# Attention into a Sinkhorn-routed expert layer: the last group's tiles in their own width, second-layer weights loaded by whole rows, five experts' weights in the first batch

## The chip, the cores and the metric

The kernel runs on one core of a Trainium2 chip. The metric is the device time of one execution in microseconds (us); several executions are timed, and the median is given. A further execution is recorded by the hardware profiler; every view of the profile and every duration below come from that one. The engines are TensorE (PE; its weight loads are shown apart as PEld), VectorE (DVE), ScalarE (ACT), GpSimd (POOL) and SyncE (SP). SP, ACT and POOL also issue transfers, each on a DMA queue of its own (q1 for SP, q10 for ACT, q0 for POOL), and all three queues run on the same 16 DMA engines.

## The reference, cut to what matters

Attention with a local window and 32 global tokens gives x, 4352 rows (8 batches x 544 positions) of 512. A small gate gives one weight per row and expert, made even over rows and columns in eight rounds. Then eight experts of two layers each are applied to all rows:

```python
    logits = x @ w_gate                      # (4352, 512) @ (512, 8)
    P = np.exp(logits - logits.max())
    for _ in range(8):
        P /= P.sum(1, keepdims=True) + 1e-09
        P /= P.sum(0, keepdims=True) + 1e-09
        P *= N / E
    for e in range(E):                       # E = 8
        h = np.maximum(x @ w1[e], 0.0)       # 512 -> 1024
        ye = h @ w2[e]                       # 1024 -> 512
        out += P[:, e:e + 1] * ye
```

The inputs are float32; the kernel computes in float16 with float32 sums.

## The kernel before, in words

**Rows and groups.** The 4352 rows are cut into nine groups m of 512, 512, ..., 256: groups 0 to 7 hold the local rows of one batch each, and the last group, m = 8 (B in the code), the 8 x 32 global rows. Activations are kept transposed, a feature in a partition and a row in a column. xT is x in this form.

**First stretch, to about 334 us: attention** for 32 pairs of heads, and mixed into it, as filling for PE, the first layer of experts 0 to 3 (`p_l1`, L459): for each group and expert eight blocks `fm` of four matmuls (L466), evicted with a relu by ACT or DVE into a tile hT of [128, 8, 512] from the pool hpool, which has four buffers. A finished tile is stored to DRAM (hd, L473) by SP, or by ACT in the second stretch. The weights w2 of the second layer are not needed yet.

**Second stretch, about 334 to 400 us.** PE still has first-layer tiles to do: `tail_run` hands them out between the rounds that make the gate even (`sk_rows`, `sk_cols`, on DVE and PE). The last four are those of group 8, experts 0 to 3 in turn; they use 256 of the 512 columns of their tile. POOL loads w2 of four experts (`load_w2c`, L665), with a cast from float32 to float16 in the transfer, and DVE makes sums of quarters (`prep_w2c`, L674).

**Third stretch, about 400 us to the end: 72 units (m, e)**, the groups in turn and in each the experts in the order ORDER = 4, 0, 5, 1, 6, 2, 7, 3. Units are numbered i from 0. An even unit is an expert of 4 to 7: its first layer is computed here (`l1`, L730: w1s from DRAM, xs is x scaled by the gate's weights pb, `scale_x`), and ACT evicts into a tile h of hpool (L738). An odd unit is an expert of 0 to 3: its h is loaded from hd by SP (`load_h`, L718) into a buffer of the same pool and scaled by DVE (`scale_h`). DVE forms `sums` of the halves of h, and PE does the second layer as seven products q of quarter blocks (`product`, L759) where eight would be the plain way. PSUM holds five of the products over all experts of a group (ps_fix); the products 6 and 7 are summed over two units in buffers of ps_rot, which has three, and added to the output tile o after each odd unit (`add`, L784; by ACT for unit 1 of a group, else by DVE, L795). The other l1 blocks use ps_rot too.

**Order.** The order of the instructions on each engine is written out by hand; the framework adds the semaphores. A buffer of a pool goes to the next tile that asks, and that tile's first writer waits for the last reader of the old one. For hpool that reader is the store of a group-8 tile. The order on DVE in the main loop matters below: at an even i it is sums(i+1), scale_x(i+4), prep_w2c of one expert (only in group 0: expert 6 at i = 0, 2 at i = 2, 7 at i = 4, 3 at i = 6), scale_h(i+3); at an odd i it is sums(i+1), then the additions. On SP: w1s of unit i+5 at an odd i; pb of units i+3 and i+4, x where a new group starts, and h of unit i+3 at an even one.

**Second-layer weights.** w2c[e] holds seven blocks of [128, 4, 256] for an expert: the four quarters of w2 and sums of them. Six experts have their tile in the pool wc, the last two of ORDER (7 and 3) in wr, which takes the place of xT once the first layer is through. After `tail_run`, POOL waits for the first group-8 tile by copying a few of its elements into a small tile `mark` (L907), then loads expert 6; a second copy into mark (L916) waits for unit 0's tile, then POOL loads experts 2, 7 and 3:

```python
    mark = wr.tile([P, 2, 2], FP16, name="mark")
    nc.gpsimd.tensor_copy(out=mark[:, 0], in_=hTs[(0, B)][:, FT - 1, 0:2])
    load_w2c(6)
```

Of the kernel before, what the change touches and what calls it, by code (L numbers as in the profile page):

```python
# [9 lines left out]
FP16 = mybir.dt.float16  # L10
FP32 = mybir.dt.float32
AF = mybir.ActivationFunctionType
ALU = mybir.AluOpType
# [10 lines left out]
def kernel(  # L24
# [13 lines left out]
    nc = tc.nc  # L38
# [51 lines left out]
    with tc.tile_pool(name="att_c", bufs=1) as att_c, \  # L90
# [368 lines left out]
        def p_l1(e, m, fm, eng, pool=None, tag="mm"):  # L459
            n = groups[m][1]  # L460
            if fm == 0:
                hTs[(e, m)] = hpool.tile([P, FT, 512], FP16, tag="hT", name="hT")
            hT = hTs[(e, m)]
            ph = (pool or ps_mm).tile([P, 512], FP32, tag=tag, name="ph")
            for dk in range(DP):
                nc.tensor.matmul(ph[:, 0:n], wts[e][:, dk, P * fm : P * (fm + 1)], xT[m][:, dk, :],  # L466
                                 start=(dk == 0), stop=(dk == DP - 1))
            if eng == "a":
                nc.scalar.activation(out=hT[:, fm, 0:n], in_=ph[:, 0:n], func=AF.Relu)  # L469
            else:  # L470
                nc.vector.tensor_scalar(out=hT[:, fm, 0:n], in0=ph[:, 0:n], scalar1=0.0, scalar2=None, op0=ALU.max)  # L471
            if fm == FT - 1:
                (nc.scalar if pool else nc.sync).dma_start(out=hd[e][m], in_=hT[:, :, 0:n])  # L473

        def load_w1e(e):
            pool, kw = ((wpool, dict(tag="w1e")), (wpool, dict(tag="w1e")), (wpool, dict(tag="w2e", bufs=1)),
# [181 lines left out]
    wc = ctx.enter_context(tc.tile_pool(name="wc", bufs=1, reuse_waits="tile"))  # L658
    xsp = ctx.enter_context(tc.tile_pool(name="xsp", bufs=2, reuse_waits="tile"))
    ORDER = (4, 0, 5, 1, 6, 2, 7, 3)  # L660
    w2c = {e: wc.tile([P, 7, FT // 2, D // 2], FP16, name=f"w2c{e}") for e in ORDER[:6]}
    idf = wc.tile([P, P], FP32, name="idf")
    HF, HD = FT // 2, D // 2

    def load_w2c(e):  # L665
        w = w2c[e]
        for i, (f, d) in ((1, (0, 0)), (4, (1, 1)), (2, (0, 1)), (3, (1, 0))):
            nc.gpsimd.dma_start(out=w[:, i], in_=moe_w2[e][P * HF * f : P * HF * (f + 1), HD * d : HD * (d + 1)]
                                .rearrange("(fko fki) d -> fki fko d", fki=P))

    def tt(out, in0, in1, op):
        nc.vector.tensor_tensor(out=out, in0=in0, in1=in1, op=op)  # L672

    def prep_w2c(e):  # L674
        w = w2c[e]
        tt(w[:, 0], w[:, 1], w[:, 4], ALU.add)
        tt(w[:, 5], w[:, 1], w[:, 2], ALU.add)
        tt(w[:, 6], w[:, 3], w[:, 4], ALU.add)
        tt(w[:, 2], w[:, 2], w[:, 4], ALU.subtract)
        tt(w[:, 3], w[:, 3], w[:, 1], ALU.subtract)  # L680

    for e in ORDER[:4]:
        load_w2c(e)

    units = [(m, e) for m in range(B + 1) for e in ORDER]
# [14 lines left out]

    def load_x(m):
        if m <= B:
            xgs[m] = xsp.tile([P, DP, 512], FP16, tag="xg", name="xg")
            nc.sync.dma_start(out=xgs[m][:, :, 0 : groups[m][1]], in_=xd[m])

    def scale_x(i):
        if i < NUN:
            m = units[i][0]
            n = groups[m][1]
            xss[i] = xsp.tile([P, DP, 512], FP16, tag="xs", name="xs")  # L710
            tt(xss[i][:, :, 0:n], xgs[m][:, :, 0:n],
               pbs.pop(i)[:, 0:n].unsqueeze(1).to_broadcast([P, DP, n]), ALU.mult)

    def alloc_h(i):
        if i < NUN:
            hs[i] = hpool.tile([P, FT, 512], FP16, tag="hT", name="h")

    def load_h(i):  # L718
        if i < NUN:
            m, e = units[i]  # L720
            alloc_h(i)
            nc.sync.dma_start(out=hs[i][:, :, 0 : groups[m][1]], in_=hd[e][m])

    def scale_h(i):
        if i < NUN:
            n = groups[units[i][0]][1]
            h = hs[i][:, :, 0:n]
            tt(h, h, pbs.pop(i)[:, 0:n].unsqueeze(1).to_broadcast([P, FT, n]), ALU.mult)

    def l1(i, fm, pool, tag):  # L730
# [32 lines left out]
    def product(i, q):  # L763
        m, e = units[i]
        n = groups[m][1]
        nt = n // P // 2
        first = e == ORDER[0]
        h, s, w = hs[i], ss[i], w2c[e]
        lhs = {1: (s[:, 2], 0), 2: (s[:, 1], 0), 3: (h[:, 0:HF], 0), 4: (h[:, HF:FT], n // 2),
               5: (s[:, 0], 0), 6: (h[:, 0:HF], n // 2), 7: (h[:, HF:FT], 0)}[q]  # L770
        if q >= 6 and i % 2 == 0:
            pm = fixed[q] = ps_rot.tile([P, 512], FP32, tag="r", name="pm")
        elif first:
            pm = fixed[q] = ps_fix.tile([P, 512], FP32, tag=f"m{q}", name=f"m{q}")
        else:
            pm = fixed[q]
        for t in range(nt):
            for k in range(HF):
                nc.tensor.matmul(pm[:, HD * t : HD * (t + 1)], lhs[0][:, k, lhs[1] + P * t : lhs[1] + P * (t + 1)],  # L779
                                 w[:, q - 1, k, :], start=(k == 0 and t == 0 and (first if q < 6 else i % 2 == 0)),  # L780
                                 stop=(k == HF - 1 and (closes(i) if q < 6 else i % 2 == 1 or closes(i))),
                                 skip_group_check=True)

# [16 lines left out]
    def last_pair(i):  # L800
        m, e = units[i]
        o, h, w = os_[m], hs[i], w2c[e]
        n = groups[m][1]
        lo, hi = h[:, 0:HF, 0:n], h[:, HF:FT, 0:n]
        s = ss[i]
        for c in range(n // P):
            q = slice(P * c, P * (c + 1))
            pm = ps_rot.tile([P, 512], FP32, tag="r", name="pm")
            for d, terms in ((1, ((lo, 2), (s, 4))), (0, ((hi, 3), (s, 1)))):
                for t, (a, wi) in enumerate(terms):  # L810
                    for k in range(HF):
                        nc.tensor.matmul(pm[:, HD * d : HD * (d + 1)], a[:, k, q], w[:, wi, k, :],
                                         start=(d == 1 and t == 0 and k == 0),
                                         stop=(t == 1 and k == HF - 1), skip_group_check=True)
            nc.vector.scalar_tensor_tensor(out=o[:, c, :], in0=pm, scalar=1.0 / float(E), in1=o[:, c, :],  # L815
                                           op0=ALU.mult, op1=ALU.add)
            for b in range(4 * c, 4 * c + 4):
                eng = {3: nc.gpsimd, 7: nc.sync}.get(b, (nc.sync, nc.scalar)[c])
                eng.dma_start(out=out[S * b : S * b + Sg, :], in_=o[W * (b % 4) : W * (b % 4 + 1), c, :])  # L819
# [79 lines left out]
    load_pb(2)  # L899
    prep_w2c(1)  # L900
    scale_x(2)
    tail_run(1000)
    load_w1(2)
    psx.close()
    wr = ctx.enter_context(tc.tile_pool(name="wr", bufs=1, side="right", reuse_waits="tile"))
    mark = wr.tile([P, 2, 2], FP16, name="mark")
    nc.gpsimd.tensor_copy(out=mark[:, 0], in_=hTs[(0, B)][:, FT - 1, 0:2])  # L907
    load_w2c(6)
    for e in ORDER[6:]:
        w2c[e] = wr.tile([P, 7, FT // 2, D // 2], FP16, name=f"w2c{e}")  # L910
    alloc_h(0)
    load_h(1)
    for fm in range(FT):
        pool, tag = cyc[fm % 2]
        l1(0, fm, pool, tag)
    nc.gpsimd.tensor_copy(out=mark[:, 1], in_=hs[0][:, FT - 1, 0:2])  # L916
    for e in (2, 7, 3):
        load_w2c(e)
    load_w1(4)
# [5 lines left out]
    for i, (m, e) in enumerate(units):  # L925
        if i == NUN - 1:
            last_pair(i)
        elif i % 2 == 0:
            alloc_h(i + 2)
            load_pb(i + 3)  # L930
            load_pb(i + 4)
            if (i + 4) % E == 0:
                load_x((i + 4) // E)
            load_h(i + 3)
            if i + 2 < NUN:
                sums(i + 1)
            else:
                n = groups[m][1]
                h = hs[i + 1]
                s = ss[i + 1] = wpool.tile([P, HF, n], FP16, tag="w2e", name="sl", bufs=1)  # L940
                tt(s, h[:, 0:HF, 0:n], h[:, HF:FT, 0:n], ALU.add)
            scale_x(i + 4)
            if m == 0:
                for e in {0: (6,), 2: (2,), 4: (7,), 6: (3,)}.get(i, ()):
                    prep_w2c(e)
            scale_h(i + 3)
            for fm in range(3):
                l1(i + 2, fm, ps_rot, "r")
            for q, fm in ((3, 3), (4, 4), (5, 5), (2, 6), (1, 7), (6, None), (7, None)):
                product(i, q)  # L950
                if fm is not None:
                    l1(i + 2, fm, ps_rot, "r")
            if closes(i):
                for q in (6, 7, 3, 4, 5, 2, 1):
                    add(i, q, fixed[q])
        else:
            load_w1(i + 5)
            sums(i + 1)
            for q in (6, 7, 3, 4, 5, 2, 1):
                product(i, q)  # L960
                if q >= 6 or closes(i):
                    add(i, q, fixed[q])
            if closes(i):
                store(m)
# [31 lines left out]
```

## Time and profile before

| what | value |
|---|---|
| three executions | 1075.87, 1077.94, 1078.65 us; median 1077.94 |
| the profiled execution | 1076.82 us, of it the span 1075.0 us from the first to the last instruction |
| mean granted TensorE clock | 0.989 of full |
| busy share of the span | PE 96%, PEld 65%, DVE 75%, ACT 45%, POOL 14% |

Busy time by stretch (us):

| stretch | length | PE | DVE | ACT | POOL | granted clock | DMA share |
|---|---|---|---|---|---|---|---|
| 0 to 334 | 334 | 310.3 | 251.3 | 260.3 | 118.7 | 0.98 | 0.79 |
| 334 to 398 | 64 | 62.9 | 44.1 | 40.6 | 17.9 | 1.00 | 0.97 |
| 398 to 461 | 63 | 51.8 | 41.9 | 18.4 | 10.1 | 0.95 | 1.02 |
| 461 to 1075 | 614 | 605.1 | 471.3 | 169.5 | 0.5 | 1.00 | 0.45 |

A stretch is read by how much PE falls short of its length: 23.7 us in the first, 1.2 in the second, 11.2 in the third and 8.9 in the last. The DMA share is a mean over the 16 engines; transfers of several queues on one engine count side by side, so it can pass 1. A time of a matmul is from its issue to its modelled end, and matmuls overlap; what a matmul costs is the distance to the next one: 0.217 us for 512 columns at full clock, 0.109 for 256.

In the chain of work that ended last, everything from 438.84 us on is one entry, "issue", of 631 us: the profile shows nothing there that the last engine waited for long.

### The profile page before, as it was taken

Reading aid. Unit: us, or ns where it says so; the run is one execution under the profiler, and the core shown is the slowest. Engines: PE = TensorE matmul, PEld = TensorE weight load, DVE = VectorE, ACT = ScalarE, POOL = GpSimd, SP = SyncE. Lnnn points to the kernel's source line nnn. Section 1 sums busy time; section 2 is a strip of 40 time slices with the busy share of each in tenths; the row PEclk is TensorE's granted clock in tenths of the full one; section 3 lists DMA queues with packets and bytes.
Section 4 is the critical chain, followed back from the end, with each engine's and each line's share of the span. In section 5 each row is a group of like instructions: output and inputs, shape, how many; then the busy total and the mean of one; then the engine's idle time right before and its main releaser. Section 6 shows DMA issues by size and latency. Waiting matters only on the chain.

```text
span 1075.0 us, 21707 instructions
## 1 busy us (share of the span) xinstructions
PE 1030.0 (96%) x8854; PEld 701.1 (65%) x8854; DVE 808.6 (75%) x1464; ACT 488.8 (45%) x1248; POOL 147.1 (14%) x233
## 2 busy tenths in 40 slices
PE   7799999999999997989999999999999999999997
PEld 4455555555554463767777777777777777777786
DVE  8577777777775763998887877878777787678766
ACT  7668888787785663223223222223223233232231
POOL 7342423413404113000000000000000000000000
PEclk9899999999999998999999999999999999999999
DMA  9877588988947979954635435435335535535351
GB/s 269 191 187 202 114 262 202 212 239 178 218 147 185 275 231 207 274 167 139 196 116 187 167 104 194 154 138 196 128 127 196 174 116 179 199 118 180 110 169 52
DMA packets 113331, 190.82 MB, mean 178 GB/s; under 512 B 33680, under 2 KB 80736, under 8 KB 100432
## 3 DMA queue, kind: packets, MB, share of 16 engines
q1 hardware_dynamic: 58176, 159.61, 43.5%
q0 software_dynamic: 48912, 20.26, 15.4%
q10 hardware_dynamic: 6144, 9.57, 2.6%
q8 instruction: 69, 1.13, 0.4%
q14 instruction: 30, 0.25, 0.1%
HBM read 157.11 MB, written 53.62 MB: 196 GB/s over the span
## 4 chain that ended last, share of the span: by engine, by line
issue 61%; PE 21%; ACT 7%; DMA 5%; DVE 5%; POOL 0%; SPq 0%; ACTq 0%; POOLq 0%
PE ph L466 14%; ACT Pu L309 4%; DVE Pu L346 2%; DMA w2c<-in_moe_w_dram 2%; DMA hd<-hT 1%; PE ptw L357 1%; ACT hT L469 1%; ACT qbd L283 1%; DMA vraw<-in_v_l_dram 1%; DMA f<-in_q_l_dram 1%; PE pt L273 1%; DMA kgf<-in_k_g_dram 1%; PE pv L155 1%; PE po L378 1%; PE sc L299 1%
## 5 line engine op out<-in xcount | busy, mean ns | idle before, releaser
L738 ACT ACTIVATE h<-ph 128x512 f16<-128x512 f32 (+1 forms) x288 | 164.8, 573 | 419.6 <-PE ph L736 404.6
L736 PE MATMUL ph<-xs,w1s 128*128 128x512 f16 (+1 forms) x1152 | 272.5, 370 | 13.0 <-ACT h L738 6.5
L466 PE MATMUL ph<-xT,w1e 128*128 128x512 f16 (+1 forms) x1152 | 257.6, 368 | 1.9 <-ACT hT L469 1.7
L779 PEld LDWEIGHTS <-h 128*128 128x128 f16 x2160 | 211.4, 98 | 44.3
L672 DVE TENSOR_TENSOR s<-h 128x1024 f16<-128x1024 f16 (+2 forms) x142 | 124.0, 915 | 103.0 <-ACT h L738 59.5
L779 PE MATMUL m<-w2c,s 128*128 128x256 f16 x1620 | 199.9, 273 | 0.0
L779 PEld LDWEIGHTS <-s 128*128 128x128 f16 x1620 | 158.4, 98 | 38.3 <-DVE s L672 0.2
L736 PEld LDWEIGHTS <-w1s 128*128 128x128 f16 x1152 | 113.3, 98 | 98.4 <-issue 17.7
L466 PEld LDWEIGHTS <-w1e 128*128 128x128 f16 x1152 | 105.5, 98 | 98.4 <-issue 6.2
L672 DVE TENSOR_TENSOR h<-h,pb 128x4096 f16<-128x4096 f16 (+1 forms) x36 | 150.7, 4186 | 4.3 <-DMA h<-hd 4.1
L779 PE MATMUL m<-w2c,h 128*128 128x256 f16 x1080 | 135.2, 273 | 0.0
L469 ACT ACTIVATE hT<-ph 128x512 f16<-128x512 f32 (+1 forms) x191 | 103.2, 559 | 50.2 <-PE ph L466 46.4
L779 PE MATMUL pm<-w2c,h 128*128 128x256 f16 x1080 | 123.8, 273 | 0.0
L672 DVE TENSOR_TENSOR xs<-xg,pb 128x2048 f16<-128x2048 f16 (+1 forms) x36 | 78.1, 2171 | 48.6 <-DMA pb<-pd 42.4
L309 ACT ACTIVATE Pu<-ms,mx 128x160 f16<-128x160 f32 x224 | 93.5, 420 | 4.0 <-DVE mx L306 1.5
L471 DVE TENSOR_SCALAR hT<-ph 128x512 f16<-128x512 f32 x97 | 66.8, 689 | 31.4 <-PE ph L466 30.8
L819 POOL DMA_DIRECT2D out_dram<-o x1 | 0.5, 534 | 638.5 <-DVE o L815 638.5
L672 DVE TENSOR_TENSOR h<-h 128x1024 f16<-128x1024 f16 (+1 forms) x142 | 87.8, 661 | 0.0
L306 DVE CUSTOM_DVE_ANT_0 ms<-sc,mask 128x160 f32<-128x160 f32 x224 | 59.9, 320 | 24.8 <-PE sc L301 22.4
L350 POOL TENSOR_TENSOR Pl<-Pu,rs 128x256 f16<-128x256 f16 x32 | 24.4, 763 | 195.9 <-DVE rs L345 130.7
L795 DVE SCALAR_TENSOR_TENSOR o<-m,o 128x512 f32<-128x512 f32 (+1 forms) x72 | 43.2, 656 | 5.2 <-ACT o L793 2.1
L346 DVE TENSOR_TENSOR Pu<-Pu,rs 128x768 f16<-128x768 f16 x64 | 44.5, 696 | 2.2
(153 smaller groups left out, 954.4 us busy)
## 6 DMA issues: line engine op xcount, KB each, us to landing
w1s<-w1d SPq DMA_DIRECT2D x36, 1024.0 KB
h<-hd SPq DMA_DIRECT2D x32, 1024.0 KB
hd<-hT SPq DMA_DIRECT2D x26, 1024.0 KB
pb<-pd SPq DMA_DIRECT2D x64, 256.0 KB
w2c<-in_moe_w_dram POOLq DMA_DIRECT2D x32, 256.0 KB, 16.1
out_dram<-o SPq DMA_DIRECT2D x8, 1024.0 KB
f<-in_q_l_dram SPq DMA_DIRECT2D x15, 512.0 KB
f<-in_k_l_dram SPq DMA_DIRECT2D x15, 512.0 KB
```

The lines of the kernel that those rows point to most:

```text
L306: nc.vector.tensor_tensor_reduce(out=ms[:, ii, :], in0=sc[:, SW * ii : SW * (ii + 1)], in1=mask[:, mi, :], scale=-scale, scalar=BIG, op0=A ...
L309: nc.scalar.activation(out=d["Pu"][:, i, :], in_=ms[:, ii, :], func=AF.Exp, scale=-1.0, bias=d["mx"][:, i : i + 1], accum_out=d["sm"][:, i ...
L346: nc.vector.tensor_tensor(out=d["Pu"][:, i0:i1, 0:KW], in0=d["Pu"][:, i0:i1, 0:KW], in1=d["rs"][:, i0:i1].unsqueeze(2).to_broadcast([P, i1 ...
L350: nc.gpsimd.tensor_tensor(out=d["Pl"], in0=d["Pu"][:, :, KW:SW], in1=d["rs"].unsqueeze(2).to_broadcast([P, NHB, Sg]), op=ALU.mult)
L466: nc.tensor.matmul(ph[:, 0:n], wts[e][:, dk, P * fm : P * (fm + 1)], xT[m][:, dk, :], start=(dk == 0), stop=(dk == DP - 1))
L469: nc.scalar.activation(out=hT[:, fm, 0:n], in_=ph[:, 0:n], func=AF.Relu)
L471: nc.vector.tensor_scalar(out=hT[:, fm, 0:n], in0=ph[:, 0:n], scalar1=0.0, scalar2=None, op0=ALU.max)
L672: nc.vector.tensor_tensor(out=out, in0=in0, in1=in1, op=op)
L736: nc.tensor.matmul(ph[:, 0:n], w1s[i][:, dk, P * fm : P * (fm + 1)], xss[i][:, dk, 0:n], start=(dk == 0), stop=(dk == DP - 1))
L738: nc.scalar.activation(out=hs[i][:, fm, 0:n], in_=ph[:, 0:n], func=AF.Relu)
L779: nc.tensor.matmul(pm[:, HD * t : HD * (t + 1)], lhs[0][:, k, lhs[1] + P * t : lhs[1] + P * (t + 1)], w[:, q - 1, k, :], start=(k == 0 and ...
L795: nc.vector.scalar_tensor_tensor(out=o, in0=p, scalar=sg / float(E), in1=o, op0=ALU.mult, op1=ALU.add)
```

## The change

Four things.

1. The tiles hT of `p_l1`, h of `alloc_h` and x of `load_x` get the width of their group, n, in place of 512. Only group 8 differs (256). A tile's rows then follow each other without gaps, so a transfer of it moves one run of 4 KB per partition (h; 2 KB for x) where it moved eight (four) of 512 bytes.
2. The blocks of w2c[e] lie in another order, [128, 4, 7, 256], so that the two quarters of a half of w2 stand side by side. `load_w2c` makes two transfers per expert of whole rows (2 KB read, 1 KB written) in place of four of half rows. `prep_w2c` and the products read the same numbers from the new places.
3. The first batch of loads takes in a fifth expert, 6; the first copy into mark and the load behind it go.
4. prep_w2c(6) moves from unit 0 of the main loop to the place after scale_x(2), ahead of the last `tail_run`.

```diff
         def p_l1(e, m, fm, eng, pool=None, tag="mm"):
             n = groups[m][1]
             if fm == 0:
-                hTs[(e, m)] = hpool.tile([P, FT, 512], FP16, tag="hT", name="hT")
+                hTs[(e, m)] = hpool.tile([P, FT, n], FP16, tag="hT", name="hT")
...
             if fm == FT - 1:
-                (nc.scalar if pool else nc.sync).dma_start(out=hd[e][m], in_=hT[:, :, 0:n])
+                (nc.scalar if pool else nc.sync).dma_start(out=hd[e][m], in_=hT)
...
-    w2c = {e: wc.tile([P, 7, FT // 2, D // 2], FP16, name=f"w2c{e}") for e in ORDER[:6]}
+    w2c = {e: wc.tile([P, FT // 2, 7, D // 2], FP16, name=f"w2c{e}") for e in ORDER[:6]}
...
     def load_w2c(e):
         w = w2c[e]
-        for i, (f, d) in ((1, (0, 0)), (4, (1, 1)), (2, (0, 1)), (3, (1, 0))):
-            nc.gpsimd.dma_start(out=w[:, i], in_=moe_w2[e][P * HF * f : P * HF * (f + 1), HD * d : HD * (d + 1)]
-                                .rearrange("(fko fki) d -> fki fko d", fki=P))
+        for f in range(2):
+            nc.gpsimd.dma_start(out=w[:, :, 1 + 2 * f : 3 + 2 * f].rearrange("p k i d -> p k (i d)"),
+                                in_=moe_w2[e][P * HF * f : P * HF * (f + 1)].rearrange("(fko fki) d -> fki fko d", fki=P))
...
     def prep_w2c(e):
         w = w2c[e]
-        tt(w[:, 0], w[:, 1], w[:, 4], ALU.add)
-        tt(w[:, 5], w[:, 1], w[:, 2], ALU.add)
-        tt(w[:, 6], w[:, 3], w[:, 4], ALU.add)
-        tt(w[:, 2], w[:, 2], w[:, 4], ALU.subtract)
-        tt(w[:, 3], w[:, 3], w[:, 1], ALU.subtract)
-
-    for e in ORDER[:4]:
+        for o, a, b, op in ((0, 1, 4, ALU.add), (5, 1, 2, ALU.add), (6, 3, 4, ALU.add),
+                            (2, 2, 4, ALU.subtract), (3, 3, 1, ALU.subtract)):
+            tt(w[:, :, o], w[:, :, a], w[:, :, b], op)
+
+    for e in ORDER[:5]:
         load_w2c(e)
...
     def load_x(m):
         if m <= B:
-            xgs[m] = xsp.tile([P, DP, 512], FP16, tag="xg", name="xg")
-            nc.sync.dma_start(out=xgs[m][:, :, 0 : groups[m][1]], in_=xd[m])
+            xgs[m] = xsp.tile([P, DP, groups[m][1]], FP16, tag="xg", name="xg")
+            nc.sync.dma_start(out=xgs[m], in_=xd[m])
...
     def alloc_h(i):
         if i < NUN:
-            hs[i] = hpool.tile([P, FT, 512], FP16, tag="hT", name="h")
+            hs[i] = hpool.tile([P, FT, groups[units[i][0]][1]], FP16, tag="hT", name="h")
...
             alloc_h(i)
-            nc.sync.dma_start(out=hs[i][:, :, 0 : groups[m][1]], in_=hd[e][m])
+            nc.sync.dma_start(out=hs[i], in_=hd[e][m])
...
-                                 w[:, q - 1, k, :], start=(k == 0 and t == 0 and (first if q < 6 else i % 2 == 0)),
+                                 w[:, k, q - 1, :], start=(k == 0 and t == 0 and (first if q < 6 else i % 2 == 0)),
...
     prep_w2c(1)
     scale_x(2)
+    prep_w2c(6)
     tail_run(1000)
     load_w1(2)
     psx.close()
     wr = ctx.enter_context(tc.tile_pool(name="wr", bufs=1, side="right", reuse_waits="tile"))
-    mark = wr.tile([P, 2, 2], FP16, name="mark")
-    nc.gpsimd.tensor_copy(out=mark[:, 0], in_=hTs[(0, B)][:, FT - 1, 0:2])
-    load_w2c(6)
+    mark = wr.tile([P, 2], FP16, name="mark")
...
-    nc.gpsimd.tensor_copy(out=mark[:, 1], in_=hs[0][:, FT - 1, 0:2])
+    nc.gpsimd.tensor_copy(out=mark, in_=hs[0][:, FT - 1, 0:2])
     for e in (2, 7, 3):
         load_w2c(e)
...
-                for e in {0: (6,), 2: (2,), 4: (7,), 6: (3,)}.get(i, ()):
+                for e in {2: (2,), 4: (7,), 6: (3,)}.get(i, ()):
                     prep_w2c(e)
```

## The prediction

> **What bounds the kernel now.** I read the waits of TensorE first, then the timelines of ACT, DVE and PE around the two largest, then the DMA queues in those stretches. PE is 96% busy. From 395 us to the end it waits five times for somebody else, 14.7 us in all:
>
> ```profile
> PE ph L736 <- ACT h L738: 6.5, 1, 6.5
> PE ph L736 <- DVE o L795: 4.7, 2, 3.0
> PE ph L736 <- DVE xs L672: 1.8, 1, 1.8
> PE ph L466 <- ACT hT L469: 1.7, 1, 1.7
> ```
>
> The 1.7 and the 6.5 lie in one place, where the first half of the expert layer ends (timelines of ACT and PE; start, duration, in brackets the idle time before and its releaser):
>
> ```profile
> 397.06 2.47 ACTq L473 DMA_DIRECT2D hd<-hT  x1
> 399.62 2.76 ACT L469 ACTIVATE hT<-ph 128x256 f16<-128x256 f32 x8 [2.60 <-issue]
> 400.06 1.91 PE L466 MATMUL ph<-xT,w1e 128*128 128x256 f16 x16 [1.71 <-ACT hT L469]
> ...
> 411.25 2.06 ACT L738 ACTIVATE h<-ph 128x512 f16<-128x512 f32 x4 [8.86 <-DMA hd<-hT]
> 411.90 8.98 PE L736 MATMUL ph<-xs,w1s 128*128 128x512 f16 x28 [6.48 <-ACT h L738]
> ```
>
> ACT sits 2.47 us in issuing the store of a last-group tile (1024 pieces of 512 B; a store of a full group takes 0.33), and PE runs out of PSUM. Then unit 0's first eviction waits for a buffer of pool hT: by the program's semaphores the one whose last-group store (expert 2) was issued at 397.06, so it landed 14 us later. PE fills four PSUM banks, idles 6.48 us and comes back at half its clock (the stretch 414 to 416; the granted clock follows POOL's column):
>
> ```profile
> 414.00:416.00 2.00, 2.00 (x6) 0.72 (x5) 0.00 (x0) 0.89 (x2) 0.00 (x0) 0.50 0.17 66
> ```
>
> 28 matmuls take 8.98 us, where 28 x 0.2167 (four in 0.867 elsewhere) are 6.07, so 2.9 more. Who holds the store up, the DMA queues from 402 to 406 say (packets, MB, busy share of 16 engines):
>
> ```profile
> q0 software_dynamic: 861, 0.42, 76.9%
> q10 hardware_dynamic: 858, 0.44, 52.8%
> ```
>
> q10 is ACT's stores, q0 POOL's load of expert 6's second-layer weights (w2c): they share the engines half and half, 215 GB/s together, until 410. The third wait, 3.0 us, is DVE's: PE lacks a bank until the addition of unit 3 (DVE timeline):
>
> ```profile
> 431.75 2.29 DVE L672 TENSOR_TENSOR xs<-xg,pb 128x2048 f16<-128x2048 f16 x1 [2.36 <-DMA pb<-pd]
> 433.96 3.10 DVE L672 TENSOR_TENSOR w2c<-w2c 128x1024 f16<-128x1024 f16 x5
> 436.97 4.42 DVE L672 TENSOR_TENSOR h<-h,pb 128x4096 f16<-128x4096 f16 x1
> ...
> 459.66 1.30 DVE L795 SCALAR_TENSOR_TENSOR o<-pm,o 128x512 f32<-128x512 f32 x2
> ```
>
> From 433.96 to there DVE has no gap, so whatever leaves that queue moves L795 forward. Between 461 and 1038 PE waits for nobody.
>
> **The change, part by part.**
>
> *Expert 6's load goes to the first batch (334 us); its mark on POOL (2.45 us) goes.* 1.05 MB leave the stretch 392 to 411. Left there are two w1s loads, two pb, four stores and one h load: 2 x 1.05 + 2 x 0.26 + 4 x 0.52 + 1.05 = 5.8 MB from 389.6 on, at 0.39 MB per us (q1 alone in 446 to 447) 15 us, so all by 404.5 and the early stores long before. In the new program unit 0 takes the buffer of expert 1's store, issued at 393.56, one store earlier than now; h of unit 1 takes that of expert 0's, issued at 390.07. I put them at 398 to 400 and 395 to 396. SP waits for the latter with w1s of unit 4, pb(3) and pb(4) queued behind it; the first of them is not due before 407, when l1 of unit 0 is through. On POOL the second load of expert 6 waits for expert 4's (the semaphores go round), and behind it stands only the mark of 407.7.
>
> *Last-group tiles in their own width.* A store is then 128 pieces of 4 KB. ACT's issue falls from 2.47 and 1.47 to some 0.35, ACT is ready for the fourth tile at 397.7, and the 1.71 goes.
>
> *Sum A.* PE runs on from 398.35: 16 narrow matmuls 1.74, 44 wide ones 44 x 0.2167 = 9.53, first product at 409.6, where it is now at 420.72: **11.1 us** = 1.71 + 6.48 + 2.9. What is late next? ACT needs its buffer at 401.0, and PE stalls only if it comes after 403.6. The second w1s is needed at 407.0 (all of q1 had landed by 402 even so far). scale_x(2) ends at 400.9, so the moved prep of w2c 6 runs 400.9 to 404.0, ahead of sums(0) at 407.7: 3.7 us of cover, then nothing. h of unit 1 is needed at 410.8 and is there by 406. If the store takes as long as now, A shrinks to 2.9 (first rival). Below nothing it can't fall: all the waits it removes are there now, and nothing is added in front of them.
>
> *Sum B: the prep leaves unit 0's DVE stretch.* Five instructions, 3.10 us, ahead of scale_h(3), which can start at 434.05 if its h is there. q1 moved 1.28 MB from 430 to 434, the pb of 0.26 and nearly all of that h, so it lands near 434.4: gain 2.7, and the stall leaves 0.3. But pb(4), issued at 426.36, moved its first byte at 430, behind q0:
>
> ```profile
> q0 software_dynamic: 396, 0.19, 144.6%
> ```
>
> (427 to 428; the rows of 425 to 429 are alike, without q1.) 395 packets of 512 B per us are 195 GB/s. The w1d loads with 2 KB packets ran 0.40 MB in 2 us (156 to 158): a cast load moves about 200 GB/s whatever its rows, so whole rows don't make w2c faster. If what stands ahead of a new transfer is a number of packets, it lasts twice as long with 1 KB packets: the 1.3 us of an undisturbed start (w1s, 418.32 to 419.7) leave 2.2 of the 3.5, so 2.2 more. Then h comes no earlier than scale_h(3) starts now, and B is 0.5 or, with pb(6) late too, -0.6. Bounds -0.6 and 2.9; neither row tells packets from bytes, so I take the middle, **1.7**.
>
> *Sum C: the last group.* Its h loads also become 4 KB pieces. DVE waits 0.31 and 0.84 us for such loads (before 1041.91 and 1049.39), ahead of the 1.66 us that PE waits for L795 at 1052. An issue falls from 0.97 to 0.35 us, the move of 0.52 MB from 1.5 (0.35 MB per us in 1048) to 1.35. I take **0.5** of bounds 0 and 1.15. The 1.84 before it waits for pb behind the output's store and stays. The Trainium skill (DMA: Bandwidth & Descriptors, Specifications) has line rate from 512 B on; by it C is 0 and the time 0.5 us longer. The trace shows 340 to 358 GB/s for these pieces against 390, a little against that rule.
>
> *At nothing.* The fifth expert in the first batch: q0 ended at 375, now 1.05 MB / 0.195 = 5.4 us later; DMA is 41% busy from 375 to 385. pd and pb(0) may come 3.5 us later, scale_x(0) at 390.7 instead of 387.2; its reader starts at 400.1. A full store's buffer is wanted four tiles, 28.8 us, later; 14.6 was the longest seen. prep on 4x256 strided: `h<-h` has that shape already, two in 1.29 us, against 15 of w2c in 9.12, no dearer. POOL's issues fall from 12 to 6 at unit 0, 0.76 each; nobody waits for POOL. The first 334 us have the same instructions.
>
> *Sum.* 11.1 + 1.7 + 0.5 = 13.3 us. The profiled execution took 1076.8 (span 1075.0, 1.8 around it), 1.1 below the median of 1077.9. 1076.8 - 13.3 = 1063.5; half the offset added, **1064**.
>
> **Rivals.**
>
> *The stores stay late.* q10 shares with two w1s loads whose 8 KB packets took 61 to 70% of the engines from 390 to 398, and 4 KB pieces may not help. For: both stores known took 14 us. Against: 8 of these were beside q0. At 14.6 us ACT starts at 408.2, PE idles 5.3 and pays the slow clock again, 2.9: A is 2.9, time 1076.8 - 2.9 - 2.2 = 1071.7.
>
> *The backlog of w2c takes the place.* POOL now issues experts 2, 7 and 3 within 4.6 us (no lane to wait for), 3.15 MB, 15.5 us at 200 GB/s. If q1 must wait for all that was issued before, pb(4) lands at 429, xs(4) ends at 431.3 where PE wants it at 426.2: 5.1 lost, and L795's stall grows by 1.0. Time 1076.8 - 11.1 + 6.1 - 0.5 = 1071.3. For: q1 moved nothing from 425 to 430. Against: at 430 q1 took 70 to 95% while q0 still had half its load to go. By the Trainium skill (DMA: Bandwidth & Descriptors, Queues, rings and completion order) the engines take turns between queues packet by packet. By it there is no backlog at all, B is 2.7 and the time 1 us shorter; the five empty rows disagree, those after 430 agree.
>
> *Slower: the product's moving operand.* The k blocks of w2c now lie 3584 B apart instead of 512. If a product's matmul (0.109 us apart, 3,812 of them) loses over 13.3 / 3812 = 3.5 ns by that, the change loses; at 6 ns it is 1063.5 + 22.9 = 1086. For: all of them read it. Against: each reads 256 contiguous columns as before, and narrow matmuls have the same 0.109 on xT (blocks 512 B apart, L466) and xs (1024 B, L736).
>
> *It does nothing*, because another wait holds unit 0 at 420: nothing in the waits names one.
>
> **Numbers.** Forecast 0.70: down to 1076.8 - 11.1 - 2.9 - 1.15 - 2.1 (the lowest run before against their median) = 1059.5, up to 1067 (A less 1, B -0.6, C 0). Late stores 0.12, backlog 0.10, slower 0.06, nothing 0.02. The range 1059.5 to 1071 holds the forecast and the better half of the two 1071 cases. What a measurement can tell here is about 0.3%, 3 us: faster 0.92, same 0.02, slower 0.06.
>
> **What would show it.** Right: no wait of PE for L738 near 400, granted clock 1.00 throughout 400 to 420, the first product near 409.6; five w2c instructions of DVE near 401; L795's wait of 3.0 under 2. Wrong in A: ACT waiting for hd; in B: DVE waiting for pb or h near 420; slower: product matmuls further apart than 0.109.

## The result, and the profile after

The changed kernel takes 1060.82 us (median of 4 runs, 1060.58 to 1062.38) against 1077.46 for the kernel before (4 runs beside it, 1075.87 to 1078.65): a ratio of 0.985, 95% interval 0.9832 to 0.9867. The profiled run took 1060.91 us with a span of 1059.1, 15.9 less than before's 1075.0. The numbers of lines are two lower behind `prep_w2c`: the eviction of h is L736, the first layer's matmul L734, the product L777, the addition L793.

What PE waits for from 395 us on (waits: total, times, longest):

```profile
PE ph L734 <- DVE o L793: 2.9, 2, 1.6
PE ph L734 <- DVE xs L672: 1.5, 1, 1.5
```

Both waits for ACT are gone; 14.7 us have become 4.4. ACT's timeline shows the seam of the two halves (start, duration; in brackets the idle time before and its releaser):

```profile
391.30 0.33 ACTq L473 DMA_DIRECT2D hd<-hT  x1
...
394.80 0.33 ACTq L473 DMA_DIRECT2D hd<-hT  x1
395.23 3.03 ACT L469 ACTIVATE hT<-ph 128x256 f16<-128x256 f32 x8 [0.46 <-PE ph L466]
398.29 0.33 ACTq L473 DMA_DIRECT2D hd<-hT  x1
399.85 2.08 ACT L736 ACTIVATE h<-ph 128x512 f16<-128x512 f32 x4 [1.59 <-DMA hd<-hT]
```

An issue takes 0.33 us where it took 2.47. ACT still waits 1.59 us for the buffer of expert 1's store (391.30 to 399.85, 8.55 us), but PE has four banks to fill meanwhile and doesn't notice (PE timeline):

```profile
394.73 3.11 PE L466 MATMUL ph<-xT,w1e 128*128 128x256 f16 x27
397.68 9.66 PE L734 MATMUL ph<-xs,w1s 128*128 128x512 f16 x44
407.17 1.04 PE L777 MATMUL m<-w2c,h 128*128 128x256 f16 x8
```

All 44 matmuls of unit 0 run in one piece, 9.66 us. The row of the stretch 398 to 445 (length, then busy time of PE, PEld, DVE, ACT, POOL; granted clock, DMA share, GB/s), first before, then after:

```profile
398.00:445.00 47.00, 38.81 (x244) 24.29 (x242) 25.94 (x22) 16.05 (x31) 10.09 (x13) 0.93 1.10 244
```

```profile
398.00:445.00 47.00, 45.88 (x324) 31.51 (x322) 40.69 (x37) 16.07 (x28) 5.64 (x7) 1.00 0.95 271
```

PE is busy 7 us more, and the clock is not cut in these 47 us. On DVE the moved operations and what now limits the addition are these (DVE timeline):

```profile
399.89 3.09 DVE L672 TENSOR_TENSOR w2c<-w2c 128x1024 f16<-128x1024 f16 x5
...
418.85 2.29 DVE L672 TENSOR_TENSOR xs<-xg,pb 128x2048 f16<-128x2048 f16 x1 [3.00 <-DMA pb<-pd]
421.98 4.43 DVE L672 TENSOR_TENSOR h<-h,pb 128x4096 f16<-128x4096 f16 x1 [0.84 <-DMA h<-hd]
...
444.70 1.28 DVE L793 SCALAR_TENSOR_TENSOR o<-pm,o 128x512 f32<-128x512 f32 x2
```

The last group keeps its two waits, a little shorter (1.84 and 1.66 before; PE timeline):

```profile
1026.42 1.47 PE L734 MATMUL ph<-xs,w1s 128*128 128x256 f16 x12 [1.50 <-DVE xs L672]
1037.99 1.03 PE L734 MATMUL ph<-xs,w1s 128*128 128x256 f16 x8 [1.37 <-DVE o L793]
```

**Where the time went.** Five marks on the timelines cut each profile into stretches: (1) until VectorE's first preparation of w2c, a stretch in which the kernels differ only in POOL's loads of w2c, from 330 us on; (2) from there to the first product; (3) to PE's restart after its first wait for the addition L795/L793; (4) to the point where PE begins to wait for xs in the last group; (5) the rest. "Wait" is PE's first wait for the addition and belongs to (3).

| profile | (1) | (2) | (3) | wait | (4) | (5) | span |
|---|---|---|---|---|---|---|---|
| before | 378.17 | 42.55 | 39.70 | 2.99 | 579.49 | 35.09 | 1075.0 |
| before, again (e9) | 377.11 | 42.40 | 40.51 | 3.73 | 581.17 | 35.21 | 1076.4 |
| changed | 375.92 | 31.25 | 38.26 | 1.56 | 579.49 | 34.18 | 1059.1 |
| changed, again (e8) | 375.40 | 31.25 | 38.71 | 2.00 | 579.49 | 33.95 | 1058.8 |
| e1 own width | 375.99 | 33.26 | 39.83 | 3.12 | 581.17 | 35.05 | 1065.3 |
| e10 the same, again | 377.49 | 33.23 | 39.67 | 2.97 | 581.12 | 34.79 | 1066.3 |
| e2 layout | 376.26 | 40.00 | 40.58 | 3.73 | 582.41 | 34.45 | 1073.7 |
| e3 earlier load and prep | 377.45 | 31.69 | 37.44 | 0.73 | 579.49 | 34.93 | 1061.0 |
| e4 changed, mark kept | 374.07 | 32.41 | 38.81 | 2.11 | 581.16 | 33.75 | 1060.2 |
| e5 changed, prep late | 377.70 | 31.25 | 40.76 | 3.73 | 581.17 | 34.42 | 1065.3 |
| e6 own width and layout | 378.29 | 35.82 | 40.45 | 3.73 | 581.18 | 34.16 | 1069.9 |
| e11 the same, again | 377.11 | 35.75 | 40.49 | 3.73 | 581.17 | 33.98 | 1068.5 |

From POOL's first load of w2c to the end of (1) it is 43.63 to 43.68 us in every profile, so what differs in (1) lies ahead of those loads. Between the two first profiles the 15.9 us are 2.25 in (1), 11.30 in (2), 1.44 in (3), nothing in (4) and 0.91 in (5). Column (2) is the forecast's step A, (3) is B, (5) is C.

### The profile page after: what moved, and what is told of

Its sections match the earlier page's. It is cut to its first block, busy times and chain, and to the rows that moved or that the text cites. A ratio compares the mean times of both kernels' runs of the same rounds, so it can differ in the third digit from the quotient of the medians.

```text
span 1059.1 us, 21691 instructions
## 1 busy us (share of the span) xinstructions
PE 1024.0 (97%) x8854; PEld 698.6 (66%) x8854; DVE 809.6 (76%) x1464; ACT 489.1 (46%) x1248; POOL 132.0 (12%) x216
## 3 DMA queue, kind: packets, MB, share of 16 engines
q0 software_dynamic: 40464, 20.26, 14.7%
## 4 chain that ended last, share of the span: by engine, by line
issue 63%; PE 21%; ACT 7%; DVE 5%; DMA 2%; POOL 1%; SPq 0%; ACTq 0%; POOLq 0%
PE ph L466 14%; ACT Pu L309 4%; DVE Pu L346 2%; ACT hT L469 1%; PE ptw L357 1%; ACT qbd L283 1%; DMA vraw<-in_v_l_dram 1%; DMA f<-in_q_l_dram 1%; DMA kgf<-in_k_g_dram 1%; PE pt L273 1%; PE ph L734 1%; PE po L378 1%; DVE m L409 1%; PE sc L299 1%; PE pt L426 1%
## 5 line engine op out<-in xcount | busy, mean ns | idle before, releaser
L736 ACT ACTIVATE h<-ph 128x512 f16<-128x512 f32 (+1 forms) x288 | 164.8, 573 | 408.4 <-PE ph L734 398.5
L734 PE MATMUL ph<-xs,w1s 128*128 128x512 f16 (+1 forms) x1152 | 269.6, 367 | 4.4 <-DVE o L793 2.9
L777 PEld LDWEIGHTS <-h 128*128 128x128 f16 x2160 | 211.4, 98 | 44.3
L777 PE MATMUL m<-w2c,s 128*128 128x256 f16 x1620 | 199.9, 273 | 0.0
L777 PEld LDWEIGHTS <-s 128*128 128x128 f16 x1620 | 158.5, 98 | 38.2
L734 PEld LDWEIGHTS <-w1s 128*128 128x128 f16 x1152 | 112.6, 98 | 87.6 <-issue 5.1
L777 PE MATMUL m<-w2c,h 128*128 128x256 f16 x1080 | 135.2, 273 | 0.0
L777 PE MATMUL pm<-w2c,h 128*128 128x256 f16 x1080 | 123.8, 273 | 0.0
L793 DVE SCALAR_TENSOR_TENSOR o<-m,o 128x512 f32<-128x512 f32 (+1 forms) x72 | 43.2, 655 | 3.8 <-ACT o L791 2.1
```

The lines of the kernel that those rows point to most:

```text
L734: nc.tensor.matmul(ph[:, 0:n], w1s[i][:, dk, P * fm : P * (fm + 1)], xss[i][:, dk, 0:n], start=(dk == 0), stop=(dk == DP - 1))
L736: nc.scalar.activation(out=hs[i][:, fm, 0:n], in_=ph[:, 0:n], func=AF.Relu)
L793: nc.vector.scalar_tensor_tensor(out=o, in0=p, scalar=sg / float(E), in1=o, op0=ALU.mult, op1=ALU.add)
```

## The experiments

**e1: own width alone.** The kernel before with the first part of the change:

```diff
-                hTs[(e, m)] = hpool.tile([P, FT, 512], FP16, tag="hT", name="hT")
+                hTs[(e, m)] = hpool.tile([P, FT, n], FP16, tag="hT", name="hT")
...
-            hs[i] = hpool.tile([P, FT, 512], FP16, tag="hT", name="h")
+            hs[i] = hpool.tile([P, FT, groups[units[i][0]][1]], FP16, tag="hT", name="h")
```

> The kernel before with the last group's tiles in their own width and nothing else: the load of expert 6 still runs beside the stores, and unit 0's h still takes expert 2's buffer. Load theory (the late 2 MB on the cast queue is what holds the stores up, piece size only adds): ACT's issues fall from 2.47 and 1.47 to about 0.33 us, but the store of expert 2 still lands after 405, PE's wait at the first unit stays above 3 us, and the run gains 2 to 5 us (1072 to 1075). Piece theory (512 B pieces that take turns with the load's packets are what made the stores slow; rows of 4 KB get most of the turns): the store lands within 8.5 us of its issue, as in the changed kernel, by about 404 to 405, PE's wait is under 3 us, and the run gains 8 to 12 us (1065 to 1069).

1068.18 us (1066.80 to 1070.07), ratio 0.9922 (0.9906 to 0.9937): 9.2 us less than before's 1077.37. The store of expert 2, with the load beside it, lands 7.7 us after its issue (ACT timeline):

```profile
394.86 0.33 ACTq L473 DMA_DIRECT2D hd<-hT  x1
395.29 3.04 ACT L469 ACTIVATE hT<-ph 128x256 f16<-128x256 f32 x8 [0.46 <-PE ph L466]
398.36 0.33 ACTq L473 DMA_DIRECT2D hd<-hT  x1
402.57 3.17 ACT L738 ACTIVATE h<-ph 128x512 f16<-128x512 f32 x6 [4.24 <-DMA hd<-hT]
```

The DMA queues from 400 to 404 say why (packets, MB, busy share of 16 engines; q10 the stores, q0 the load):

```profile
q10 hardware_dynamic: 261, 0.93, 61.5%
q0 software_dynamic: 492, 0.24, 44.6%
```

Before, the two queues had the same number of packets, 858 to 861 (402 to 406), and so the same bytes. A piece of 4 KB carries eight times as much per packet, and the store moves 0.93 MB in the 4 us where it moved 0.44. The load theory falls for these tiles: the load need not go for the store to be quick. From 398 to 400 the packets are even here too, 63 of the store, 66 of the load and 68 of SP's loads; why they are 261 to 492 from 400 on isn't shown.

**e2: layout alone.**

```diff
-    w2c = {e: wc.tile([P, 7, FT // 2, D // 2], FP16, name=f"w2c{e}") for e in ORDER[:6]}
+    w2c = {e: wc.tile([P, FT // 2, 7, D // 2], FP16, name=f"w2c{e}") for e in ORDER[:6]}
...
-        for i, (f, d) in ((1, (0, 0)), (4, (1, 1)), (2, (0, 1)), (3, (1, 0))):
+        for f in range(2):
...
-                                 w[:, q - 1, k, :], start=(k == 0 and t == 0 and (first if q < 6 else i % 2 == 0)),
+                                 w[:, k, q - 1, :], start=(k == 0 and t == 0 and (first if q < 6 else i % 2 == 0)),
```

> The kernel before with the second-layer weights' new layout and whole-row loads and nothing else. Prediction: the cast queue writes about 200 GB/s with 512 B and with 1 KB rows, so the time stays within 2 us of before (1075 to 1079). Rival, packets take turns: the load's 1 KB packets now take twice the bytes of the store's 512 B pieces in the shared stretch, the store of expert 2 lands 2 to 4 us later than 411 and the run is 2 to 4 us slower. Rival, issue cost: fewer issues on POOL bring something: 1 to 3 us faster.

1075.99 us (12 runs, 1070.00 to 1077.23), ratio 0.998 (0.9964 to 0.9996): 1.4 us less than before, within what the forecast said. The rival in which the store is held longer falls: expert 2's store takes 13.1 us (395.13 to 408.26) where it took 14.2 (397.06 to 411.25), and the first product comes 2.5 us sooner (ACT timeline, then the queues from 402 to 406):

```profile
395.13 2.68 ACTq L473 DMA_DIRECT2D hd<-hT  x1
...
408.26 2.06 ACT L736 ACTIVATE h<-ph 128x512 f16<-128x512 f32 x4 [7.58 <-DMA hd<-hT]
```

```profile
q0 software_dynamic: 560, 0.54, 79.9%
q10 hardware_dynamic: 663, 0.34, 38.8%
```

The load moves 0.54 MB where it moved 0.42, so it is done sooner, and the rest of the store has the engines to itself (1366 packets against 4 from 406 to 408). The 1.4 us also lie in the range of the issue rival; what the trace shows of the gain is the store's, and PE's waits from 390 us on name ACT and DVE, never POOL.

**e3: the earlier load and preparation alone**, with the old layout and the old widths:

```diff
-    for e in ORDER[:4]:
+    for e in ORDER[:5]:
...
+    prep_w2c(6)
     tail_run(1000)
...
-    nc.gpsimd.tensor_copy(out=mark[:, 0], in_=hTs[(0, B)][:, FT - 1, 0:2])
-    load_w2c(6)
...
-                for e in {0: (6,), 2: (2,), 4: (7,), 6: (3,)}.get(i, ()):
+                for e in {2: (2,), 4: (7,), 6: (3,)}.get(i, ()):
```

> The kernel before with expert 6 loaded in the first batch, its mark copy gone and its five DVE operations ahead of the first unit, old layout and old tile widths (stores in 512 B pieces). Load theory: with no cast load beside them the stores land within about 10 us of their issue, unit 0's h (now in expert 1's buffer) is free by about 403, PE waits 0 to 3 us there, and the run gains 9 to 13 us (1064 to 1068) plus the 1.4 us of the shorter stretch of VectorE. Piece theory: 512 B pieces keep the issues at 0.6 to 2.5 us and the stores slow; gain under 6 us (above 1071).

1062.49 us (1061.95 to 1064.25), ratio 0.987 (0.9856 to 0.9884): 14.9 us less, a little more than expected. The stores are still of 512 B pieces, but no cast load is there to take turns with (DMA queue, 398 to 402):

```profile
q10 hardware_dynamic: 1537, 0.77, 64.0%
```

1537 packets in 4 us against 349 before in those four. Issues take 0.55 to 1.04 us and expert 1's store 9.2 (392.83 to 402.07), so PE waits 0.28 us and the first product is 31.69 behind the preparation. The piece theory, that small pieces alone are slow, falls too. Each half of the change alone takes most of column (2): 9.3 us by the pieces, 10.9 by the load, 11.3 by both. (Of the 10.9 and the 11.3, 1.2 go with the earlier buffer, as e4 measures it.) What cost the time was their meeting.

**e4: which buffer unit 0 gets.** The changed kernel with a small copy that lengthens the life of expert 4's last tile:

```diff
-    mark = wr.tile([P, 2], FP16, name="mark")
+    mark = wr.tile([P, 2, 2], FP16, name="mark")
+    nc.gpsimd.tensor_copy(out=mark[:, 0], in_=hTs[(0, B)][:, FT - 1, 0:2])
```

> The changed kernel with the first of POOL's two mark copies kept (of 128x2 elements, no load behind it): it lengthens the life of expert 4's last tile, so that unit 0's h takes the buffer of expert 2's store and not of expert 1's; everything else is as in the changed kernel. Buffer theory: that store is issued 3.5 us later (394.80) and, at the 8.5 us that expert 1's took, lands at 403.3; ScalarE waits 5.0 instead of 1.6 us, of which PE's four banks cover some 0.8 more, so PE waits about 2.7 us and the run is 2.5 to 5.5 us slower than the changed kernel (1063.5 to 1066.5; the upper end if the clock drops after the stall). Traffic theory (the buffer is of no account once the load is gone): within 1 us of the changed kernel.

1062.81 us (1061.94 to 1064.23), 2.0 more than the changed kernel's median and 1.1 more than its second one (e8, 1061.72). By the time alone the two theories can't be told apart, so the profile has to decide, and it is in part as the buffer theory says. Expert 2's store took 6.9 us and not 8.5 (392.94 to 399.79), so PE waits 1.00 where 2.7 were expected (PE timeline):

```profile
400.44 6.20 PE L734 MATMUL ph<-xs,w1s 128*128 128x512 f16 x28 [1.00 <-ACT h L736]
...
445.29 2.49 PE L734 MATMUL ph<-xs,w1s 128*128 128x512 f16 x8 [2.11 <-DVE o L793]
```

Column (2) is 1.16 longer: that is what one store earlier is worth here. The second line shows a longer wait for the addition, 2.11, and a cut clock behind it: the eight matmuls take 2.49 us where they take 1.89 after a shorter wait.

**e5: the preparation put back.**

```diff
-    prep_w2c(6)
     tail_run(1000)
...
-                for e in {2: (2,), 4: (7,), 6: (3,)}.get(i, ()):
+                for e in {0: (6,), 2: (2,), 4: (7,), 6: (3,)}.get(i, ()):
```

> The changed kernel with only the five DVE operations of expert 6 put back into the first unit, behind the scaling of unit 4's x; the weights are still loaded in the first batch. Theory of the stretch (3.09 us on VectorE ahead of the adds; of these, 0.84 lie in its present wait for h): PE's wait for the adds grows from 1.56 to about 3.8 us, and the granted clock drops behind it, as it did in the run with the old load (3.1 to 3.7 us of wait): 1063 to 1066.5. Rival (the wait shrank because the late load was gone, and not because of the operations): the wait stays under 2 us and the run within 1 us of the changed kernel.

1065.64 us (1064.67 to 1067.08), 3.9 more than the changed kernel in the same comparison (1061.72). The wait and the clock behind it (PE timeline, then the rows of two stretches):

```profile
449.71 2.85 PE L734 MATMUL ph<-xs,w1s 128*128 128x512 f16 x8 [3.73 <-DVE o L793]
```

```profile
450.00:454.00 4.00, 4.00 (x17) 2.03 (x16) 4.00 (x6) 1.19 (x2) 0.00 (x0) 0.57 0.77 317
454.00:458.00 4.00, 4.00 (x29) 2.63 (x27) 4.00 (x6) 1.20 (x2) 0.00 (x0) 1.00 0.01 2
```

The granted clock is 0.57 for four microseconds, PE issues 17 matmuls instead of 29, and column (4) is 581.17 instead of 579.49: 1.68 us. The rival falls: the wait is DVE's five operations. All eight profiles with the late preparation have 2.97 to 3.73 us there, the four of the table without it 0.73 to 2.11.

**e6: own width and layout**, the diffs of e1 and e2 together; the load stays late.

> The kernel before with own-width tiles and the new layout of the second-layer weights; expert 6 is still loaded late. Both readings of the first run (rows of 4 KB take their turns beside the load) expect the first product about 33 us after VectorE's first preparation, as there (33.26), and PE's wait for h at 1 to 2.5 us; the rival that 1 KB cast packets hold a store up twice as long as 512 B ones expects 35 us or more. Time 1065 to 1070, by the clock behind the wait for the adds.

1070.44 us (1066.16 to 1071.75), ratio 0.9933 (0.9910 to 0.9956), just above the range. The rival was right: 35.82, and a wait of 2.72 us with a cut clock behind it (28 matmuls in 7.89 us, 6.20 in e1). Packets from 400 to 404, and PE:

```profile
q1 hardware_dynamic: 119, 0.87, 54.0%
q10 hardware_dynamic: 136, 0.49, 30.5%
q0 software_dynamic: 136, 0.14, 20.4%
```

```profile
406.38 7.89 PE L734 MATMUL ph<-xs,w1s 128*128 128x512 f16 x28 [2.72 <-ACT h L736]
```

The store and the load are again even in packets, and SP's loads on q1 nearly so. The store of expert 2 takes 8.57 us (397.16 to 405.73) where it took 7.71 in e1.

**e7: a faster version.** What the changed kernel still waits for is pb: with two buffers pb(4) can be issued only when the scaling of unit 1's h is over (412.78; the issue is at 412.81), h of unit 3 stands behind it on SP, and in the last group pb stands behind an output store.

```diff
-            pbs[i] = xsp.tile([P, 512], FP32, tag="pb", name="pb")
+            pbs[i] = xsp.tile([P, 512], FP32, tag="pb", name="pb", bufs=3)
...
-    idf = wc.tile([P, P], FP32, name="idf")
+    idf = skp.tile([P, P], FP32, tag="dg", name="idf", bufs=1)
...
     load_w1(2)
+    load_pb(4)
     psx.close()
...
             alloc_h(i + 2)
-            load_pb(i + 3)
-            load_pb(i + 4)
-            if (i + 4) % E == 0:
-                load_x((i + 4) // E)
             load_h(i + 3)
+            if i == 0:
+                load_pb(3)
...
+            load_pb(i + 5)
+            load_pb(i + 4)
+            if (i + 5) % E == 0:
+                load_x((i + 5) // E)
             load_w1(i + 5)
```

> An attempt at a faster version. The changed kernel with three pb buffers instead of two (idf takes dg's place, one srs), pb(4) loaded ahead of the first unit, later pb and x loads issued at the head of each odd unit (ahead of a group's output store), and h ahead of pb(3). Theory (what is left at the first unit and in the last group is pb arriving late: VectorE idle 3.00 and 5.61 us for it): the waits of 1.56, 1.50 and 1.37 us go, together 4.4: 1055.5 to 1058. Rival (the loads only trade places in the queue, h or the weights come later by as much): within 1 us of the changed kernel, 1060 to 1062.

1054.07 us (1052.70 to 1056.07), ratio to before 0.9789 (0.9772 to 0.9807), against 0.9863 (0.9844 to 0.9882) for the changed kernel in the same comparison; it is 1.4 below the range expected. Of the waits of PE from 395 us on this is left, near the end:

```profile
PE ph L733 <- DVE o L792: 0.6, 1, 0.6
```

DVE runs on without a gap where it waited 3.00 and 0.84 us:

```profile
412.34 1.83 DVE L671 TENSOR_TENSOR s<-h 128x2048 f16<-128x2048 f16 x2
414.09 1.29 DVE L671 TENSOR_TENSOR h<-h 128x1024 f16<-128x1024 f16 x2
415.29 2.28 DVE L671 TENSOR_TENSOR xs<-xg,pb 128x2048 f16<-128x2048 f16 x1
417.49 4.42 DVE L671 TENSOR_TENSOR h<-h,pb 128x4096 f16<-128x4096 f16 x1
```

The span is 1054.3, 4.5 less than e8's 1058.8, where the waits removed are 4.5 - 0.6 = 3.9 (e8 has 2.00, 1.24 and 1.30). So the theory holds and the rival falls. The medians differ by 7.7, more than the profiles: clock cuts that the changed kernel met in its other runs may be the rest, but these runs have no profile, and it stays open.

**e8: the changed kernel again.**

> The changed kernel once more, as it is. Of the 15.9 us between the two first profiles, 2.26 were there before the first instruction that the change moves (VectorE's first preparation at 375.92, before at 378.17). Chance theory (the clock grants of the attention stage vary from run to run): this profile has the preparation anywhere between 374 and 378.5 and the time moves with it, 1060 to 1063. Rival (the changed program is really earlier there): again within 0.5 us of 375.9.

1061.72 us (1060.55 to 1064.69), preparation at 375.40. Alone this would suit the rival, but e5, with the same instructions up to there, has 377.70, and e4 374.07. Over the table's profiles the mark lies anywhere from 374.07 to 378.29, with no order by kernel. The clock goes with it: in the first 60 us the granted clock is at half for 3.4 us in the trace with the earliest mark (e4) and for 13.7 us in the two with the latest (before, e6).

**e9 to e11: three second profiles** of before, e1 and e6.

> The kernel before, a second profile. Chance theory of the early clock: VectorE's first preparation anywhere between 374 and 378.5 (378.17 in the first profile); the first product 42.5 us behind it (420.72 there), within 1.5, since the store beside the load decides that and not the clock of the attention stage. Rival (the load's and the store's place against each other is itself a matter of chance): the distance differs by more than 3 us.

Preparation at 377.11, first product 42.40 behind it: as expected. But this execution paid more at the addition than the first one did (PE timeline):

```profile
411.00 8.68 PE L736 MATMUL ph<-xs,w1s 128*128 128x512 f16 x28 [6.58 <-ACT h L738]
...
460.02 3.23 PE L736 MATMUL ph<-xs,w1s 128*128 128x512 f16 x8 [3.73 <-DVE o L795]
```

A wait of 3.73 and a cut clock (column (4) 581.17), which the first profile, the one the forecast was made from, had not: 2.99, and 579.49.

> The own-width tiles alone, a second profile: if what decides is turns of packets, the store of expert 2 takes 7.7 us again from its issue to ScalarE's first eviction (within 0.5) and the first product comes 33.3 us after the first preparation.

> Own width and new layout, a second profile: if 1 KB cast packets hold a store up longer than 512 B ones, the store of expert 2 takes 8.6 us again (7.7 with 512 B packets), PE waits 2.5 us or more for h; if that was chance, the store takes about 7.7 here too.

7.66 us for expert 2's store with 512 B cast packets (396.37 to 404.03) and 8.49 with 1 KB (395.99 to 404.48): repeated, as are the waits (1.82 and 2.65). The larger cast packets do hold a store of 4 KB pieces up, by 0.85 us.

## Why the prediction was right, point by point

The forecast was 1064 with 1059.5 to 1071; measured 1060.8. It rests on a sum of 13.3 us; the profiles show 13.65 in the stretches it spoke of (11.30, 1.44, 0.91) and 2.25 in one that it took to be the same.

- **Step A, 11.1 us: 11.3.** The stores' estimates held: expert 1's buffer free at 399.85 (398 to 400 said), expert 0's store followed by SP's next load at 395.68 (395 to 396), the moved preparation over at 402.98, ahead of the sums at 405.41. The slow clock was 2.9 and went with the wait, as booked. What the text gave as the cause, the load that shares the engines half and half, is only half of it: e1 gets 9.3 us with the load in place. The first rival's ground, that 4 KB pieces may not help, falls with the same run. Among the parts, the earlier buffer brings 1.16 (e4); the forecast counted it without a price.
- **Step B, 1.7 us: 1.4 in the first pair of profiles, 1.8 in the second (40.51 to 38.71).** The size held by chance: the middle of the bounds given, -0.6 and 2.9, is 1.15, and 1.7 is that of 0.5 and 2.9 (and from 436.97 to 434.4 it is 2.6, not the 2.7 given). The step "the stall leaves 0.3" failed: 1.56 or 2.00 are left, and 0.73 with the old layout (e3). The forecast asked whether the queue ahead is counted in packets or bytes. In the changed kernel pb(4) moves its first byte 3.5 us after its issue at 412.81, as long as before (3.6), so nothing doubled; what holds the first byte back stays open. But the larger packets do cost something behind it: unit 4's x is scaled 6.0 to 6.5 us after that issue in the seven profiles with the new layout, and 5.4 to 5.5 in four of the five with the old one (6.2 in e9). So the layout takes back a part of what the moved preparation brings: column (3) is 37.44 in e3 and 38.26 to 38.81 in the changed kernel and e4. Also, pb(4) is issued late, behind the scaling of unit 1's h; e7, with a third buffer and another order of the loads, has no wait there. The term that was left out is the clock: behind the longer wait it is cut in e9, e5 and e1, for 1.68 us each. That is why e5 costs 3.9 and not 2.
- **Step C, 0.5 us: 0.9, for another reason.** Against the first profile of before, own width alone brings 0.04 and 0.3 in column (5), the layout alone 0.64. So the forecast's piece sizes are a third of it at most. The Trainium skill (DMA: Bandwidth & Descriptors, Specifications: line rate from 512 B) fits this better than the trace's row that was set against it. "The 1.84 stays" was wrong: 1.50 and 1.24. The wait is 1.24 to 1.59 in six profiles with the layout (1.77 in e5) and 1.74 to 1.95 in the five without. With the layout it begins 7.06 us after the output store's issue (7.05 in e2) and without it 6.70 (6.71 in e1 and e3); why the store is issued 0.36 us sooner stays open.
- **At nothing.** The strided preparation takes 9.11 us (9.12); unit 0's x is scaled 10.29 us behind the first preparation instead of 9.03, 1.3 late and not 3.5, and it is hidden; and no wait of PE shows the fifth load. All held.
- **Slower, by the product's operand:** falls. Column (4), which holds nearly all the products, is 579.49 us in both, to the hundredth.
- **The backlog of w2c:** falls; q1 takes its turns from 416 on, and PE waits for no xs at unit 2.
- **The 2.25 us ahead of everything** were no part of the sum. They are not the change's: the granted clock from 36 to 60 us was 0.80 in before's profile and 0.93 in the changed kernel's, and the mark of column (1) moves by 4.2 us over the profiles. The medians' 16.6 us hold, besides 13.65, the same kind of chance and the cut behind the addition that before meets in some executions and the changed kernel met in neither of its profiles. How often each does over all runs wasn't measured.

## What to carry to other kernels

When two queues meet, ask how many packets each has and not only how many bytes: a transfer of small pieces beside a cast load of small packets goes at one packet for one. Larger pieces or moving the load away are two cures for one illness, so price them together and not as a sum. And add to a wait of TensorE of some 2 us and more the clock that may be cut behind it, by chance of where the wait falls; then look at which buffer a late load is waiting for before its queue is blamed.

## What the runs showed of the hardware

- **Queues take turns by packets.** 861 to 858 with 512 B on both sides, 136 to 136 with 1 KB against 4 KB, 63 to 66 to 68 on three queues (e1, 398 to 400). The Trainium skill (DMA: Bandwidth & Descriptors, Queues, rings and completion order) says that each engine goes round its queues packet by packet; the trace agrees in these stretches. In e1 from 400 on, 261 to 492, it doesn't, and why isn't shown.
- **An issue grows with the pieces and with the load beside it.** The same 0.5 MB store takes ACT 0.33 us in 128 pieces of 4 KB; in 1024 pieces of 512 B 0.55 to 1.04 without the cast load (e3) and up to 2.68 beside the cast load (e2).
- **The clock is cut after short waits, and it matters where they fall.** It stayed whole behind PE's waits of 0.73, 1.00, 1.56, 1.82, 1.85 and 2.00 us, and was cut behind 1.95 (e1, last group), 2.11, 2.65, 2.72, 2.97, 3.12, five of 3.73, 5.20, 6.48 and 6.58; one of 2.99 (before, first profile) went free. The clock records of the thirteen traces sort this. Up to the last few microseconds every cut of a trace is one or two stretches of 3.41 us, all on one grid. From 60 us on, where PE was idle for 1.95 us or more of such a stretch at full clock, the next one ran at half (14 times); where it was idle for 1.90 or less, none did. The two nearest cases, each a stretch and the next one (busy time of PE first, granted clock behind POOL's column), are e1's wait of 1.95, which lies in one stretch, and before's of 2.99, which falls into two as 1.09 and 1.90:

```profile
1029.55:1032.97 3.42, 1.47 (x15) 1.10 (x13) 2.02 (x2) 0.09 (x1) 0.00 (x0) 1.00 1.00 411
1032.97:1036.38 3.41, 3.41 (x19) 2.43 (x17) 3.41 (x6) 1.44 (x4) 0.00 (x0) 0.50 0.42 126
```

```profile
458.52:461.93 3.41, 1.51 (x8) 0.68 (x8) 3.41 (x6) 0.46 (x1) 0.00 (x0) 1.00 0.98 231
461.93:465.34 3.41, 3.41 (x25) 2.35 (x24) 3.41 (x5) 1.34 (x3) 0.00 (x0) 1.00 0.67 284
```

A cut of one stretch behind the addition costs 1.6 to 1.7 us; in e2 it is two stretches, and column (4) is 2.92 longer. The Trainium skill (TensorE: Matmul & The Clock Gate, What's actually happening) has the clock halved after an idle window of about 3.4 us whose bounds run freely. The traces agree on the length and on the bounds; they don't bear out that a whole window must be idle, as 1.95 us of it are enough.
